# The last output tile of a TensorE-bound kernel: two equal column pieces, or a wide and a narrow one with its copy on VectorE

## The chip, the cores and the metric

The kernel runs on one core of one Trainium2 chip. The metric is the time of one execution on the device, in microseconds (us); lower is better. Each kernel is executed several times, and kernels of one set run on the same chip in turn with the kernel before.

The *execution time* is what is compared. The *span* is the stretch from the first to the last of the program's own instructions in the profile. The profile prints the span to 0.1 us; where two or three decimals are given below, they come from the trace behind it. "Outside the span" below is the execution time of the profiled execution minus the span of that same execution.

## The reference

Normalised linear attention over 8 batches of 576 tokens, 8 heads of 64, and then two matrix products with an ELU between them (4608 tokens, 512 to 2048 to 512):

```python
kv  = einsum('bhsd,bhse->bhde', k, v)
out = einsum('bhsd,bhde->bhse', q, kv)
rms = sqrt(mean(out * out, axis=-1, keepdims=True) + 1e-06)
x   = (out / rms * g_norm)            # then (b, h, s, d) -> (b*s, h*d)
h   = x @ w_in                        # 4608 x 2048
g   = where(h > 0, h, exp(min(h, 0)) - 1)
y   = g @ w_out                       # 4608 x 512
```

## The kernel before

The tokens are worked off in nine groups of 512; in each, TensorE makes `h` (lines with `h_ps`), ScalarE and VectorE make the ELU, and TensorE makes the output (`o_ps`). The change touches only the end: the output of the last group. Its four tiles of 128 tokens x 512 columns need 16 accumulating matmuls each. The last tile is already cut into two column pieces of 256, so that the copy and the store of the first piece overlap the matmuls of the second:

```python
    rows = out.rearrange("(i l s) f -> l s i f", l=2, s=S)
    pieces = [(j, slice(0, DM)) for j in range(J - 1)]
    pieces += [(J - 1, slice(0, DM // 2)), (J - 1, slice(DM // 2, DM))]
    for j, cols in pieces:
        n = cols.stop - cols.start
        ps = ps_m2.tile([P, DM], FP32, name="o_ps", tag="mm2")[:, 0:n]
        for f in range(FC):                       # FC = 16
            nc.tensor.matmul(ps, lhsT=gT[B][:, f, j * P : j * P + P],
                             rhs=w_out_sb[:, f, cols], start=(f == 0), stop=(f == FC - 1))
        sb = outp.tile([P, DM], FP32, name="o_last", tag="o_last", bufs=5)[:, 0:n]
        nc.scalar.copy(sb, ps)
        for l, eng in enumerate((nc.sync, nc.scalar)):
            eng.dma_start(out=rows[l, G:S, j, cols], in_=sb[l * 64 : l * 64 + 64, :])
```

Two small VectorE instructions of the start play a part later:

```python
    one = const.tile([1, 1], FP32, name="one")
    nc.vector.memset(one, 1.0)
    # ... read by one small matmul near 8 us
```

Of the kernel before, what the change touches and what calls it, by code (L numbers as in the profile page):

```python
# [8 lines left out]
FP32 = mybir.dt.float32  # L9
# [7 lines left out]
def kernel(  # L17
# [13 lines left out]
    nc = tc.nc  # L31
    P = 128

    B, H, S, D = q.shape
    DM = H * D
    DF = moe_w_in.shape[1]
    NPAIR = H // 2
    J = 4
# [13 lines left out]
    outp = ctx.enter_context(tc.tile_pool(name="outp", bufs=3))  # L52
# [452 lines left out]
    for s in range(2):  # L505
# [7 lines left out]
        out=g_row,  # L513
        in_=bass.AP(tensor=g_norm.tensor, offset=g_norm.offset, ap=[[1, 1], [0, 2], [1, 64]]),
# [160 lines left out]
    for l in range(2):  # L675
        ls = slice(l * 64, l * 64 + 64)
        nc.gpsimd.tensor_copy(
            out=bd_kv[ls, 0].rearrange("p (s u) e -> p u s e", s=2)[:, :, :, ls], in_=kv0[ls]
# [117 lines left out]
            ahead["qd"]()  # L796
    rows = out.rearrange("(i l s) f -> l s i f", l=2, s=S)
    pieces = [(j, slice(0, DM)) for j in range(J - 1)]
    pieces += [(J - 1, slice(0, DM // 2)), (J - 1, slice(DM // 2, DM))]
    for j, cols in pieces:  # L800
        n = cols.stop - cols.start
        ps = ps_m2.tile([P, DM], FP32, name="o_ps", tag="mm2")[:, 0:n]
        for f in range(FC):
            nc.tensor.matmul(  # L804
                ps,
                lhsT=gT[B][:, f, j * P : j * P + P],
                rhs=w_out_sb[:, f, cols],
                start=(f == 0),
                stop=(f == FC - 1),
            )  # L810
        sb = outp.tile([P, DM], FP32, name="o_last", tag="o_last", bufs=5)[:, 0:n]
        nc.scalar.copy(sb, ps)
        for l, eng in enumerate((nc.sync, nc.scalar)):
            eng.dma_start(out=rows[l, G:S, j, cols], in_=sb[l * 64 : l * 64 + 64, :])

# [29 lines left out]
```

## Time and profile before

| what | value | view |
|---|---|---|
| execution time | 287.24 us, median of 3 (287.07 to 287.27) | times |
| TensorE busy | 98% of the span | busy table |
| last matmul ends (modelled) | 283.62 us | trace |
| last copy, ScalarE, 256 columns | 283.66 us, 0.372 us | timeline, groups |
| last two stores issued | 284.06 us | timeline |
| both landed | 286.27 us | trace |
| end of the span | 287.24 us | trace |

So 3.62 us lie between the end of the last matmul and the end of the span. They are called the *tail* here.

These are lines of the page of the kernel before: span, TensorE's busy time, the granted TensorE clock in 40 slices (tenths of full speed), and the chain that ended last, by engine.

```profile
span 287.2 us, 4859 instructions
...
PE 280.8 (98%) x2001; PEld 134.8 (47%) x2001; DVE 168.8 (59%) x220; ACT 144.1 (50%) x205; POOL 53.5 (19%) x94
...
PEclk9689999999999999999999999999999999999999
...
PE 97%; ACT 1%; DVE 0%; issue 0%
```

TensorE is the bound. Note the 6 and the 8 at the start of the clock row: in this one execution the granted clock was 0.50 from about 9.8 to 16.7 us (0.68 and 0.84 as means of those two slices). That execution took 289.14 us, not 287.24, so its early part is not typical; its tail is.

The end of the timeline of the kernel before; the columns are start in us, duration in us, engine, line, operation, operands, and in brackets the idle time before it and what ended that.

```profile
start us, us, engine line op out<-in xcount [idle before <-releaser]
...
281.91 0.37 ACT L812 COPY o_last<-o_ps 128x256 f32<-128x256 f32 x1 [1.16 <-PE o_ps L804]
282.31 0.50 ACTq L814 DMA_DIRECT2D out_dram<-o_last  x1
283.66 0.37 ACT L812 COPY o_last<-o_ps 128x256 f32<-128x256 f32 x1 [1.38 <-PE o_ps L804]
284.06 0.50 ACTq L814 DMA_DIRECT2D out_dram<-o_last  x1
```

The two copies start 1.75 us apart, which is 16 matmuls of 109 ns. ScalarE waits for TensorE before each.

From the groups of instructions of the kernel before (busy us, mean ns of one, idle before): what copies of other sizes take.

```profile
L812 ACT COPY o_last<-o_ps 128x512 f32<-128x512 f32 x3 | 1.8, 586 | 8.2 <-PE o_ps L804 8.2
...
L812 ACT COPY o_last<-o_ps 128x256 f32<-128x256 f32 x2 | 0.7, 372 | 2.5 <-PE o_ps L804 2.5
L579 DVE COPY r<-bank 128x512 f32<-128x512 f32 x1 | 0.7, 692 | 0.8 <-PE bank L567 0.8
...
L608 DVE COPY g_col<-bank 128x1 f32<-128x1 f32 x1 | 0.2, 157 | 0.3 <-PE bank L601 0.3
```

And the stores of the last tiles among its DMA issues (size, median us from issue to landing):

```profile
out_dram<-o_last SPq DMA_DIRECT2D x3, 128.0 KB, 2.4
out_dram<-o_last ACTq DMA_DIRECT2D x3, 128.0 KB, 2.7
...
out_dram<-o_last SPq DMA_DIRECT2D x2, 64.0 KB, 1.9
out_dram<-o_last ACTq DMA_DIRECT2D x2, 64.0 KB, 2.2
```

Halving the bytes of a store took only 0.5 us off 2.4 to 2.7. Most of it did not change with the size.

### The profile page before, as it was taken

How to read it: one execution, taken by the hardware profiler on the slowest of the kernel's cores; microseconds unless marked ns; L12 is line 12 of the kernel's file. 1: busy time of each engine (PE TensorE's matmuls, PEld its weight loads, DVE VectorE, ACT ScalarE, POOL GpSimd, SP SyncE). 2: the span in 40 equal slices, each digit the busy share in tenths (PEclk: the TensorE clock that was granted, in tenths of full speed). 3: DMA queues.
4: the chain of work that ended last, by engine and by line, in shares of the span. 5: the costliest groups of instructions: out<-in, count | busy, mean ns of one | idle time of the engine just before them, and what ended most of it. 6: DMA issues, size and time to landing. Idle time of an engine off the chain costs nothing.

```text
span 287.2 us, 4859 instructions
## 1 busy us (share of the span) xinstructions
PE 280.8 (98%) x2001; PEld 134.8 (47%) x2001; DVE 168.8 (59%) x220; ACT 144.1 (50%) x205; POOL 53.5 (19%) x94
## 2 busy tenths in 40 slices
PE   7999999999999999999999999999999999999994
PEld 3444445444554454445444544454444444444444
DVE  5348752589368657755775477538764776444400
ACT  3569744685496455445543554345534553333311
POOL 7726302431421151005200520012000000000000
PEclk9689999999999999999999999999999999999999
DMA  7999999795896599258925892544251213010122
GB/s 197 204 206 203 207 204 156 222 195 116 136 176 76 147 130 219 39 146 108 219 59 147 100 232 50 147 91 137 47 139 36 85 29 109 0 75 0 73 73 73
DMA packets 55961, 35.96 MB, mean 125 GB/s; under 512 B 32772, under 2 KB 53508, under 8 KB 55940
## 3 DMA queue, kind: packets, MB, share of 16 engines
q0 software_dynamic: 20192, 17.30, 38.9%
q1 hardware_dynamic: 35348, 17.83, 24.6%
q10 hardware_dynamic: 400, 0.52, 0.5%
q8 instruction: 15, 0.25, 0.3%
q14 instruction: 6, 0.05, 0.0%
HBM read 36.70 MB, written 9.44 MB: 161 GB/s over the span
## 4 chain that ended last, share of the span: by engine, by line
PE 97%; ACT 1%; DVE 0%; issue 0%
PE h_ps L399 42%; PE o_ps L446 39%; PE o_ps L804 5%; PE bank L527 3%; PE at L208 2%; PE at L177 2%; PE kv_ps L177 1%; PE at L659 1%; PE h_ps L659 1%; PE bank L567 1%; PE bank L196 1%; PE at L306 0%; PE bank L583 0%; PE at L217 0%; PE at L188 0%; PE se_ps L208 0%
## 5 line engine op out<-in xcount | busy, mean ns | idle before, releaser
L399 PE MATMUL h_ps<-xT,w_in_sb 128*128 128x512 bf16 x560 | 130.9, 379 | 0.0
L446 PE MATMUL o_ps<-w_out_sb,gT 128*128 128x512 bf16 x512 | 120.5, 379 | 0.0
L411 ACT ACTIVATE elu_e<-h_ps 128x1024 bf16<-128x1024 f32 (+1 forms) x75 | 73.0, 982 | 81.8 <-PE h_ps L399 80.1
L399 PEld LDWEIGHTS <-w_in_sb 128*128 128x128 bf16 x560 | 53.6, 98 | 62.0 <-issue 0.2
L430 DVE TENSOR_TENSOR gT<-elu_e,h_ps 128x1024 bf16<-128x1024 bf16 (+1 forms) x66 | 76.3, 1157 | 6.9
L446 PEld LDWEIGHTS <-gT 128*128 128x128 bf16 x512 | 49.8, 98 | 59.0
L422 DVE TENSOR_SCALAR elu_e<-elu_e 128x1024 bf16<-128x1024 bf16 (+1 forms) x76 | 32.7, 430 | 70.7 <-ACT elu_e L411 70.5
L459 ACT COPY o_sb<-o_ps 128x512 f32<-128x512 f32 x32 | 18.6, 587 | 16.4 <-PE o_ps L446 16.4
L232 DVE TENSOR_REDUCE ss<-sq 128x16 f32<-128x1024 bf16 x16 | 19.3, 1218 | 8.7 <-ACT sq L227 8.7
L227 ACT ACTIVATE sq<-at 128x1024 bf16<-128x1024 f32 x14 | 14.3, 1024 | 12.4 <-PE at L208 9.9
L151 POOL COPY q_bf<-q_pk 128x512 bf16<-128x512 bf16 x24 | 14.5, 632 | 28.7 <-DMA q_pk<-in_q_dram 28.7
L242 DVE TENSOR_TENSOR xs<-at,ss 128x1024 bf16<-128x1024 f32 x14 | 17.1, 1218 | 1.2 <-ACT ss L239 1.2
L804 PE MATMUL o_ps<-w_out_sb,gT 128*128 128x512 bf16 (+1 forms) x80 | 14.1, 337 | 0.0
L125 POOL COPY gate<-qT 1x1 bf16<-1x1 bf16 x6 | 1.1, 184 | 63.2 <-DMA qT<-q_bf 63.2
L104 POOL DMA_DIRECT2D q_pk<-in_q_dram x14 | 10.7, 772 | 2.9 <-issue 1.9
L804 PEld LDWEIGHTS <-gT 128*128 128x128 bf16 x80 | 7.8, 98 | 6.4 <-DVE gT L430 0.4
L527 PE MATMUL bank<-zeros 128*128 128x512 bf16 x19 | 8.5, 587 | 1.2 <-DVE zeros L502 1.2
L118 POOL DMA_DIRECT2D k_pk<-in_k_dram x12 | 8.4, 700 | 5.8 <-DMA w_in_sb<-in_moe_w_in_dram 2.9
L417 ACT ACTIVATE elu_h<-h_ps 128x1024 bf16<-128x1024 f32 x9 | 9.2, 1019 | 0.0
L177 PEld LDWEIGHTS <-k_pk 64*64 64x64 bf16 x576 | 7.0, 110 | 4.2 <-issue 4.0
L208 PEld LDWEIGHTS <-qT 128*128 128x128 bf16 x112 | 7.3, 98 | 3.5 <-issue 0.5
L118 POOL DMA_DIRECT2D v_pk<-in_v_dram x12 | 8.4, 698 | 2.3 <-DMA w_in_sb<-in_moe_w_in_dram 1.8
(71 smaller groups left out, 116.4 us busy)
## 6 DMA issues: line engine op xcount, KB each, us to landing
out_dram<-o_sb SPq DMA_DIRECT2D x16, 512.0 KB, 3.0
q_pk<-in_q_dram POOLq DMA_DIRECT2D x14, 256.0 KB, 5.2
k_pk<-in_k_dram POOLq DMA_DIRECT2D x6, 576.0 KB, 8.2
v_pk<-in_v_dram POOLq DMA_DIRECT2D x6, 576.0 KB, 10.5
w_in_sb<-in_moe_w_in_dram POOLq DMA_DIRECT2D x4, 512.0 KB, 11.1
w_out_sb<-in_moe_w_out_dram POOLq DMA_DIRECT2D x4, 512.0 KB, 14.7
st_q<-in_q_dram SPq DMA_DIRECT2D x2, 512.0 KB, 4.7
st_q<-in_q_dram SPq DMA_DIRECT2D x16, 64.0 KB, 2.5
```

The source lines that it names most:

```text
L118: nc.gpsimd.dma_start(out=raw[name, b].rearrange("p h j d -> p h (j d)")[:, hs], in_=in_[:, hs])
L177: nc.tensor.matmul(kv_ps[l * 64 : l * 64 + 64, s, u * 64 : u * 64 + 64], lhsT=bf["k", T][rows, j, 2 * u + l, :], rhs=bf["v", T][rows, j, 2 ...
L232: nc.vector.reduce_sum(out=ss, in_=sq.rearrange("p c (h e) -> p (c h) e", h=H), axis=AX.X)
L242: nc.vector.tensor_tensor(out=xs.rearrange("p c (h e) -> p (c h) e", h=H), in0=se_ps.rearrange("p c (h e) -> p (c h) e", h=H), in1=ss.to_b ...
L399: nc.tensor.matmul(h_ps[a][:, cs], lhsT=w_in_sb[:, c, f * P : f * P + P], rhs=x(c, cs), start=(c == 0), stop=(c == KC - 1),)
L411: nc.scalar.activation(e[:, lo:hi, :], ps, AF.Exp)
L422: nc.vector.tensor_scalar(out=e[:, lo:hi, :], in0=e[:, lo:hi, :], scalar1=1.0, scalar2=1.0, op0=ALU.min, op1=ALU.subtract,)
L430: nc.vector.tensor_tensor(out=gT[T][:, 2 * i + lo : 2 * i + hi, :], in0=e[:, lo:hi, :], in1=h, op=ALU.add if relu else ALU.max,)
L446: nc.tensor.matmul(o_ps[T, j], lhsT=gT[T][:, f, j * P : j * P + P], rhs=w_out_sb[:, f, :], start=(f == 0), stop=(f == FC - 1),)
L459: nc.scalar.copy(o_sb[T][:, j % 2, :], o_ps.pop((T, j)))
L527: nc.tensor.matmul(ps, lhsT=zeros[:, 0:P], rhs=zeros, start=True, stop=True)
L804: nc.tensor.matmul(ps, lhsT=gT[B][:, f, j * P : j * P + P], rhs=w_out_sb[:, f, cols], start=(f == 0), stop=(f == FC - 1),)
```

## The change

The intent is a shorter tail: a narrower last piece needs a shorter copy and a smaller last store. VectorE makes the last copy, because ScalarE would still be busy with the copy and the DMA issue of the wide piece.

```diff
-    pieces += [(J - 1, slice(0, DM // 2)), (J - 1, slice(DM // 2, DM))]
+    pieces += [(J - 1, slice(lo, hi)) for lo, hi in ((0, 384), (384, 512))]
 ...
-        sb = outp.tile([P, DM], FP32, name="o_last", tag="o_last", bufs=5)[:, 0:n]
-        nc.scalar.copy(sb, ps)
+        sb = outp.tile([P, DM], FP32, name="o_last", tag="o_last", bufs=6)[:, 0:n]
+        if cols.stop == DM and n < DM:
+            nc.vector.tensor_copy(out=sb, in_=ps)
+        else:
+            nc.scalar.copy(sb, ps)
```

## The prediction

> **What bounds the kernel now.** TensorE. The busy table has PE at 280.8 of 287.2 us (98%), and the chain of waits is 97% PE. Only the tail after the last matmul is not PE. In the timeline the last tile's two 256-column pieces end 1.745 us apart (ScalarE copies at 281.91 and 283.66), 109 ns per matmul. After the last matmul: copy 0.372 us from 283.66, two DMA issues at 284.06 (SP and ACT queues), landing near 286.27 (1.9 to 2.2 us after issue, DMA table), then about 0.97 us of closing semaphores to 287.24. Of these 3.6 us only the copy and the data part of the DMA can shrink.
>
> **What the change removes, adds, moves.**
> 1. PE: 32 matmuls stay 32. A 128-wide one takes 56 ns elsewhere (the chain: eight in 0.45 us), so weight loads keep up. [...]this trace agrees at 512 (1.73 us / 8 = 216 ns), 256 (109) and 128 (56), so 384 should be 162.5. Estimate: 16 x (162.5 + 56) = 3.50 us against 3.49. Neutral; last matmul still ends at about 283.63.
> 2. Last copy: 128 columns instead of 256, on VectorE. Two VectorE copies from PSUM in this trace: 512 f32 columns 692 ns, 1 column 157 ns; so about 290 ns for 128 (a 128-column cast takes 288). Against 372: saves 0.08 us. On ScalarE the 128 columns would take about 265 ns (586 for 512, 372 for 256), but ScalarE would be busy: the 384 copy (about 0.48 us) plus its DMA issue (0.50) reach past the 0.90 us of the last piece by about 0.15 us. VectorE, idle since 272.6 us, avoids that. The engine choice only protects the gain.
> 3. Last DMA: half the bytes, 512-byte rows. Data of a 512-wide piece moved in about 1.14 us, of a 256-wide in about 0.73 (the trace's packets); so about 0.55 for 128: up to 0.18 us less. But the 384 piece, issued near 283.32, moves from about 284.4 to 285.4, and the last piece, issued near 283.98, starts moving near 285.1: they overlap by about 0.3 us on the same DMA engines, which may eat most of that. Net 0 to 0.15 us.
> 4. A sixth output buffer; nothing else moves in the instruction order.
>
> **On the critical path:** 0.08 us of copy and about 0.06 us of DMA. Sum about -0.14 us, 0.05% of the run, less than the spread of three runs (0.20 us).
>
> **Predicted time:** 287.10 us; 8 in 10 between 286.85 and 287.35. Faster by over 2%: 0.005; within 2%: 0.99; slower by over 2%: 0.005.
>
> **What would show each step right:** PE busy and the start of the last copy unchanged within 0.03 us (1); a VectorE copy of 280 to 300 ns as last link of the chain, with its DMA issues at about 283.98, no wait on a busy queue (2); landing of the last pieces at 286.05 to 286.25, with packets of the 384 piece still moving when the last ones begin (3).
>
> **What would make it wrong:** weight loads not keeping up through sixteen 128-wide matmuls (each 10 ns over 56 costs 0.16 us); the 384 piece's data holding up the last one by over 0.3 us, which turns the gain into a small loss; run-to-run drift larger than the effect.

The 162.5 ns for 384 columns stays as an estimate: it lies midway between the 109 ns at 256 columns and the 216 ns at 512 in the profile before.

## The result

| | before | changed |
|---|---|---|
| execution time, median of 6 | 287.24 us (287.07 to 287.38) | 287.38 us (287.21 to 287.46) |
| ratio changed / before, 95% interval | | 1.0005 (0.9992 to 1.0018) |

A ratio here and below is the mean time of one kernel's fast runs over that of the other's of the same rounds, so not quite the ratio of the medians. The result is not the gain of 0.14 us that was predicted, and it lies 0.03 us above the predicted range.

The page of the changed kernel, the same rows:

```profile
span 285.4 us, 4859 instructions
...
PE 277.7 (97%) x2001; PEld 133.2 (47%) x2001; DVE 168.4 (59%) x221; ACT 143.7 (50%) x204; POOL 53.3 (19%) x94
...
PEclk9999999999999999999999999999999999999999
...
PE 88%; DMA 10%; issue 0%; ACT 0%; DVE 0%; POOLq 0%
```

The span is 1.8 us shorter, but that must not be credited to the change: this profile caught full clock all through, the other did not. With full clock the chain starts with the loading of the weights ("DMA 10%") instead of TensorE work. That is a property of the execution. The kernel before, profiled again later (run before_again below), had full clock too, and its page shows the shorter span and the same chain:

```profile
span 285.5 us, 4859 instructions
...
PE 88%; DMA 10%; issue 0%; ACT 0%; POOLq 0%
```

The end of the timeline of the changed kernel:

```profile
start us, us, engine line op out<-in xcount [idle before <-releaser]
...
281.09 0.48 ACT L815 COPY o_last<-o_ps 128x384 f32<-128x384 f32 x1 [2.01 <-PE o_ps L804]
281.60 1.39 ACTq L817 DMA_DIRECT2D out_dram<-o_last  x2
281.98 0.29 DVE L813 COPY o_last<-o_ps 128x128 f32<-128x128 f32 x1 [11.10 <-PE o_ps L804]
```

Its stores of the last tile, to set beside those of before:

```profile
out_dram<-o_last SPq DMA_DIRECT2D x1, 96.0 KB
out_dram<-o_last ACTq DMA_DIRECT2D x1, 96.0 KB, 2.4
out_dram<-o_last SPq DMA_DIRECT2D x1, 32.0 KB, 2.0
out_dram<-o_last ACTq DMA_DIRECT2D x1, 32.0 KB, 2.1
```

The steps of the tail came out close to the prediction, except for one DMA issue (below). The last tile takes TensorE 3.657 us against 3.656 (matmuls of 384 columns start 162.5 ns apart, those of 128 columns 56 ns). The VectorE copy takes 292 ns. From the issue on the ACT queue to the moment when SyncE sees both stores landed, 2.154 us pass against 2.212. The tail is 3.474 us against 3.620. So 0.15 us were gained where they were sought, and the execution is still not shorter. Something else must cost about as much or more.

The exception is the last DMA issue on the ACT queue. The timeline above merges it with the issue before it; alone it is

```profile
282.31 0.68 ACTq L817 DMA_DIRECT2D out_dram<-o_last  x1
```

It took 0.68 us, against 0.50 in the kernel before. The prediction had "no wait on a busy queue" here. What that costs shows in split_act below.

A first pointer was in the runs themselves. The six executions of the changed kernel took 1.99 to 2.06 us longer than their spans (spans known to 0.1 us), where the one profiled execution of the kernel before took 1.90 us longer.

### The profile page after: what moved, and what is told of

Same layout as the page of the kernel before. It is cut to its first block, busy times and chain, and to the rows that moved or that the text cites. A ratio compares the mean times of both kernels' runs of the same rounds, so it can differ in the third digit from the quotient of the medians.

```text
span 285.4 us, 4859 instructions
## 1 busy us (share of the span) xinstructions
PE 277.7 (97%) x2001; PEld 133.2 (47%) x2001; DVE 168.4 (59%) x221; ACT 143.7 (50%) x204; POOL 53.3 (19%) x94
## 4 chain that ended last, share of the span: by engine, by line
PE 88%; DMA 10%; issue 0%; ACT 0%; DVE 0%; POOLq 0%
PE h_ps L399 39%; PE o_ps L446 39%; DMA w_out_sb<-in_moe_w_out_dram 6%; PE o_ps L804 5%; DMA w_in_sb<-in_moe_w_in_dram 3%; PE at L208 2%; DMA k_pk<-in_k_dram 2%; PE at L177 2%; PE at L306 0%; PE at L217 0%; PE se_ps L208 0%; ACT bd_kv L356 0%; PE xt_ps L306 0%; DVE o_last L813 0%; POOLq L832 0%
## 5 line engine op out<-in xcount | busy, mean ns | idle before, releaser
L422 DVE TENSOR_SCALAR elu_e<-elu_e 128x1024 bf16<-128x1024 bf16 (+1 forms) x76 | 31.8, 419 | 71.6 <-ACT elu_e L411 71.6
L804 PE MATMUL o_ps<-w_out_sb,gT 128*128 128x512 bf16 (+2 forms) x80 | 14.1, 337 | 0.0
L430 DVE TENSOR_TENSOR gT<-elu_e,elu_h 128x1024 bf16<-128x1024 bf16 x9 | 6.6, 735 | 2.9 <-ACT elu_h L417 2.4
```

Of the source, the lines that this page charges most:

```text
L422: nc.vector.tensor_scalar(out=e[:, lo:hi, :], in0=e[:, lo:hi, :], scalar1=1.0, scalar2=1.0, op0=ALU.min, op1=ALU.subtract,)
L430: nc.vector.tensor_tensor(out=gT[T][:, 2 * i + lo : 2 * i + hi, :], in0=e[:, lo:hi, :], in1=h, op=ALU.add if relu else ALU.max,)
L804: nc.tensor.matmul(ps, lhsT=gT[B][:, f, j * P : j * P + P], rhs=w_out_sb[:, f, cols], start=(f == 0), stop=(f == FC - 1),)
```

## The experiments

The theories as they stood, in order:

- A: the total is only scatter of the part before the tail; with more runs the 0.14 us gain would show.
- B: something before the tail became slower, for example by moved addresses of the larger pool.
- C: the time outside the span became longer. Within it, C1: it depends on how many instructions VectorE has; C2: it depends on VectorE working late.

dve_plus9, dve_plus2, dve_plus5, dve_plus129, dve_plus128 and act_extra were single looks, whose state is unknown; only their tail and their time outside the span are used, not their totals. "Tail" is from the modelled end of the last matmul to the end of the span. Medians are of the same set; "before" in each set is that set's own runs of the kernel before, on the same chip. The five sets ran on chips 15, 8, 11, 14 and 15.

### First set: is it scatter, is it the pool, does the tail count at all?

**before_again**: no edit.

> The kernel before, unchanged, against itself. It measures how far two sets of runs of one kernel lie apart. Theory A (the change shortens the tail by 0.14 us, and the +0.14 us of the first timing is scatter of the part before the tail): medians of the two sets may differ by up to 0.15 us, single runs spread over 0.2 to 0.4 us. Theory B (the changed kernel really is about 0.14 us slower): the two sets agree within 0.05 us. In the profile, both theories: from the start of the last copy to the end 3.58 us, as in the first profile.

Measured: 287.40 us median of 6 against 287.35 of 11 runs of the same kernel; ratio 1.0012 (0.9966 to 1.0058). Tail 3.595 us. Outside the span 1.797 us. Single runs spread from 287.04 to 291.19 us. The medians of one kernel agree within 0.05 us here, but single runs go astray far more. Theory B falls here in its general form, as far as one profile of each kernel can tell: with full clock the last matmul ended at 281.95 us in this run and at 281.95 us in the first profile of the changed kernel.

**after_again**: the changed kernel, no edit.

> The changed kernel, unchanged, timed with more rounds. Theory A: 0.0 to 0.3 us below the kernel before (-0.14 expected), with the scatter of single runs larger than that. Theory B (something outside the tail costs about 0.28 us and outweighs the tail): +0.14 us again, interval clear of zero. Profile, both: VectorE copy 290 ns, from the start of the last copy to the end 3.44 us.

Measured: 287.60 us of 6 against 287.35; ratio 1.0010 (0.9971 to 1.0048). Tail 3.467 us, again 0.14 us shorter. Outside the span 1.992 us, 0.20 more than in the run of the kernel before beside it. The second set of timings has the changed kernel above the kernel before too, though no interval excludes equality.

**six_buffers**

```diff
-        sb = outp.tile([P, DM], FP32, name="o_last", tag="o_last", bufs=5)[:, 0:n]
+        sb = outp.tile([P, DM], FP32, name="o_last", tag="o_last", bufs=6)[:, 0:n]
```

> The kernel before with six output buffers in place of five, nothing else; the sixth is never used. Theory A: within 0.1 us of the kernel before. Theory B, in the form that the larger pool or its moved addresses cost the time: +0.14 to +0.28 us. Tail from the last copy's start to the end unchanged at 3.58 us.

Measured: 287.40 us against 287.35; ratio 0.9999 (0.9967 to 1.0032). Tail 3.601 us, outside the span 1.768 us. The buffer is not the cause; theory B falls in that form too.

**one_piece**

```diff
-    pieces += [(J - 1, slice(0, DM // 2)), (J - 1, slice(DM // 2, DM))]
+    pieces += [(J - 1, slice(0, DM))]
```

> The last tile in one piece of 512 columns, copied by ScalarE: the same term of the sum made larger the other way, as a check that a longer tail reaches the total one for one. Copy 0.586 us in place of 0.372 (+0.21), the data of the last DMA 1.14 us in place of 0.73 (up to +0.4): tail 4.1 to 4.2 us from the start of the last copy, total +0.5 to +0.65 us. Both theories expect this; if the total moved by less than +0.3 us, the tail would not be on the critical path as assumed.

Measured: 287.97 us against 287.35 (+0.62); ratio 1.0025 (0.9988 to 1.0061), so the total alone is not clear of noise. The tail is 4.374 us, 0.77 more than the 3.61 us of before. Outside the span 1.772 us. By the medians a longer tail reaches most of the total, so a shorter one should as well.

### Second set: what lies outside the span

**split_act**: the last copy of the changed kernel back on ScalarE.

```diff
-        if cols.stop == DM and n < DM:
-            nc.vector.tensor_copy(out=sb, in_=ps)
-        else:
-            nc.scalar.copy(sb, ps)
+        nc.scalar.copy(sb, ps)
```

> The changed kernel with its last copy on ScalarE instead of VectorE. So far the profile shows the tail 0.14 us shorter with the change, while the total is not shorter; what the total has beyond the profiled span was 2.0 us in all runs of the changed kernel, and 1.77 to 1.90 us in the four kernels without the VectorE copy. Theory C: that part outside the span belongs to the VectorE copy and hides the gain. It expects here 1.77 to 1.90 us outside the span. Theory A (scatter only) expects no pattern. Tail, both: the last copy can't start before ScalarE has issued the 384 piece's DMA, so it starts about 0.15 us after its last matmul and takes 265 ns; tail counted from the last matmul about 0.1 us longer than with VectorE, about as before.

Measured: 287.09 us of 5 against 287.26 of 11; ratio 0.9988 (0.9966 to 1.0010). Outside the span 1.768 us. Tail 3.499 us, better than expected. The end of its timeline:

```profile
280.97 0.48 ACT L812 COPY o_last<-o_ps 128x384 f32<-128x384 f32 x1 [2.01 <-PE o_ps L804]
281.48 0.50 ACTq L814 DMA_DIRECT2D out_dram<-o_last  x1
282.02 0.27 ACT L812 COPY o_last<-o_ps 128x128 f32<-128x128 f32 x1 [0.57 <-PE o_ps L804]
282.31 0.55 ACTq L814 DMA_DIRECT2D out_dram<-o_last  x1
```

The last matmul ended at 281.82 us and the copy began at 282.02, once the DMA issue was off ScalarE's queue (281.48 + 0.50). So ScalarE really is late, by 0.16 us (the usual gap is 0.04). But its copy is 26 ns shorter, and the tail is still 0.11 us shorter than before. VectorE's part in the change is worth only about 0.03 us of tail. The record shows why it is so little. In the changed kernel the last issue on the ACT queue starts 0.13 us earlier after the last matmul (0.36 us against 0.49), but it takes 0.68 us instead of 0.55, so both end 1.04 us after the last matmul. In these traces this issue took 0.67 to 0.68 us when it started 0.71 us after the issue before it (five runs), 0.55 us at 0.84 us and 0.50 us at 0.95 us or more. The reason isn't shown.

**halves_dve**

```diff
 (from the changed kernel)
-    pieces += [(J - 1, slice(lo, hi)) for lo, hi in ((0, 384), (384, 512))]
+    pieces += [(J - 1, slice(lo, hi)) for lo, hi in ((0, 256), (256, 512))]
```

> Two pieces of 256 as in the kernel before, the last copied by VectorE (and six buffers). VectorE copy 256 columns about 425 ns (157 + 256 x 1.045), against 372 on ScalarE: tail +0.05 us, 3.61 to 3.64 us from the copy's start. Theory C: 2.0 us outside the span, total +0.25 us. Theory A: no pattern, total +0.05 us.

Measured: 287.59 us of 6 against 287.26; ratio 1.0015 (0.9990 to 1.0041). Copy 425 ns, tail 3.663 us, outside the span 2.008 us. The cost outside came with VectorE's copy, not with the sizes of the pieces.

**dve_extra**: one more VectorE instruction that has nothing to do with the tail.

```diff
 (from the kernel before, ahead of "rows = ...")
+    nc.vector.memset(const.tile([P, 1], FP32, name="unused"), 0.0)
```

> The kernel before with one more VectorE instruction, a memset of one unused column that nobody waits for, placed after VectorE's last real work; tail 3.56 to 3.58 us as before. Theory C1 (VectorE's instruction count is what costs outside the span): 2.0 us outside, total +0.2 us. Theory C2 (that VectorE is still at work when the kernel ends): 1.77 to 1.90 us outside, total unchanged. Theory A: unchanged.

Measured: outside the span 2.013 us. VectorE's last lines in its timeline:

```profile
269.97 1.22 DVE L430 TENSOR_TENSOR gT<-elu_e,h_ps 128x1024 bf16<-128x1024 bf16 x1
271.14 0.06 DVE L797 MEMSET unused<- 128x1 f32 x1
```

VectorE is done at 271.2 us of a span of 285.9, and nobody waits for the memset. Yet the time outside the span grew just as it does with the VectorE copy. C2 falls: late work is not the cause. The total was 287.74 us of 5 against 287.26, more than expected; in the profiled execution 0.3 us of it is a later last matmul (282.25 us, against 281.95 in before_again). That is taken here for scatter of the part before the tail. It isn't shown: four of the five spans were 285.7 us or more, against a median of 285.5 for the kernel before in this set.

**dve_even**: the changed kernel with one VectorE memset moved away. This one went wrong.

```diff
 (from the changed kernel)
-    nc.vector.memset(one, 1.0)
+    nc.gpsimd.memset(one, 1.0)
```

> The changed kernel with one early VectorE memset of one element moved to GpSimd, so that VectorE has as many instructions as in the kernel before. Tail 3.43 to 3.44 us as in the changed kernel. Theory C1: 1.77 to 1.90 us outside the span, total -0.14 us against before. Theory C2: 2.0 us outside, total +0.05 us. Theory A: -0.14 us give or take 0.15.

Measured: 301.61 us, 14 us slower. The memset had to queue behind the DMA issues of GpSimd: in the profile it ran at 20.30 us, right after a DMA issue of 0.71 us that began at 19.59. A small matmul reads it, at 8.4 us in the kernel before and at 20.4 us here. The lines of that matmul's view: what its engine sat idle for, and who waited for it.

```profile
its engine sat idle before it (us, times) until:
  POOL one L508: 24.3, 2
who waited for it (us, times):
  DVE g_col L608: 12.7, 1
```

The 24.3 us are 12.2 us of the weight load and 12.1 us of the matmul, at the same time. The total is useless, an error of the experiment. Its tail (3.455 us) and the time outside the span (1.767 us) can still be read, and they favour C1. The edit was repeated in a clean form.

### Third set: the count, and better versions

**dve_const**

```diff
 (from the changed kernel)
-    one = const.tile([1, 1], FP32, name="one")
-    nc.vector.memset(one, 1.0)
+    one = nc.const_aps.tensor(1.0, (1, 1), FP32)
```

> The changed kernel with the one-element VectorE memset of 1.0 left out; its reader takes the 1.0 that the framework has already put in memory at the start. VectorE then has 309 instructions in the trace as in the kernel before, and still makes the last copy. (The attempt before, with that memset moved to GpSimd, stalled TensorE for 12 us at the start and its total says nothing; its tail was 3.42 us and the part outside the span 1.77 us.) Theory C1: 1.77 us outside the span, tail 3.43 us, total 0.10 to 0.20 us below the kernel before. Theory C2 (late VectorE work costs): 2.0 us outside, total +0.05 us.

Measured: 287.14 us of 5 against 287.29 of 9; ratio 0.9988 (0.9967 to 1.0009). Tail 3.469 us, outside the span 1.782 us. With one VectorE instruction fewer at the very start of the program, the changed kernel shows its gain in the medians.

**dve_plus9**: nine unused memsets in the place of the one of dve_extra.

```diff
 (from the kernel before; n = 9, and below n = 2, 5, 128, 129)
+    unused = const.tile([P, n], FP32, name="unused")
+    for c in range(n):
+        nc.vector.memset(unused[:, c : c + 1], 0.0)
```

> The kernel before with nine more VectorE memsets that nobody waits for, in the place of the one of the earlier experiment (318 VectorE instructions). If each instruction costs outside the span: 1.77 + 9 x 0.24 = 3.9 us. If it is a step at one more instruction than before (309 to 310): 2.0 us, as with one more.

Measured: outside the span 1.796 us. Neither of the two forms expected: nine more instructions cost nothing outside the span, though one more costs 0.24 us. So it is neither a price for each instruction nor a step that stays.

**act_extra**

```diff
 (from the kernel before)
+    nc.scalar.copy(const.tile([P, 1], FP32, name="unused"), eps_col)
```

> The kernel before with one more ScalarE instruction (a copy of one column that nobody waits for), VectorE at 309. If the cost outside the span comes with VectorE's own count: 1.77 us. If it comes with the program's total count or with any engine: 2.0 us.

Measured: outside the span 1.810 us. One more instruction in total, or one more on ScalarE at this place, does not bring the cost; with dve_extra beside it, the effect belongs to VectorE's count.

**act_352**: an attempt to beat both kernels without VectorE.

```diff
 (from split_act)
-    pieces += [(J - 1, slice(lo, hi)) for lo, hi in ((0, 384), (384, 512))]
+    pieces += [(J - 1, slice(lo, hi)) for lo, hi in ((0, 352), (352, 512))]
```

> A version meant to beat both: pieces of 352 and 160 columns, all copied by ScalarE. The last piece's matmuls take [...]1.11 us, longer than ScalarE needs for the copy of 352 (0.45 us) and the DMA issue (0.50) with their gaps, so the last copy (292 ns) starts as soon as its matmuls end, 0.04 us after. Theory C1: 1.77 us outside the span, tail from the last matmul about 3.44 us against 3.60 before and 3.50 with 384 and 128 on ScalarE; total 0.15 to 0.2 us below the kernel before.

The 1.11 us stands as an estimate from the 56 ns at 128 columns and the 109 ns at 256 of the profile before: about 69 ns at 160, times 16. In the run the two last copies start 1.11 us apart.

Measured: 287.08 us of 5 against 287.29 of 9; ratio 0.9984 (0.9960 to 1.0008). Outside the span 1.776 us, tail 3.414 us.

```profile
280.82 0.45 ACT L812 COPY o_last<-o_ps 128x352 f32<-128x352 f32 x1 [1.80 <-PE o_ps L804]
281.30 0.50 ACTq L814 DMA_DIRECT2D out_dram<-o_last  x1
281.93 0.29 ACT L812 COPY o_last<-o_ps 128x160 f32<-128x160 f32 x1 [0.66 <-PE o_ps L804]
282.25 0.50 ACTq L814 DMA_DIRECT2D out_dram<-o_last  x1
```

The last matmul ended at 281.89 us, and the copy started 0.04 us later: the last piece is just wide enough for ScalarE to have its DMA issue behind it, and the last issue takes 0.50 us again. In the tail it gives the whole gain of the change, with no VectorE at all.

### Fourth and fifth set: one unlucky count, or a step that recurs?

**dve_plus2**: n = 2.

> The kernel before with two unused VectorE memsets (311 VectorE instructions). Outside the span so far: 309 gives 1.77 to 1.80 us (one first look 1.90), 310 gives 1.99 to 2.01 in four kernels, 318 gives 1.80. If only a single count is hit: 1.77 us. If a stretch of counts from 310 up to somewhere under 318 is hit, with the cost fading as the count grows: 1.9 to 2.0 us.

Measured: outside the span 2.100 us.

**dve_plus5**: n = 5.

> The same with five unused memsets (314 VectorE instructions). Single count: 1.77 us. Fading stretch: 1.8 to 1.95 us.

Measured: outside the span 1.865 us. With 2.10 at two and 1.80 at nine, it is a stretch of counts over which the cost fades.

**dve_plus129**: n = 129, which is 128 more than dve_extra.

> The same with 129 unused memsets (438 = 310 + 128 VectorE instructions[...]). If the cost comes[...]: 2.0 us again. If not[...]: 1.77 to 1.80 us. The memsets take about 9 us of VectorE time and end before the last matmul, so the tail stays at 3.56 to 3.60 us.

To test: 2.0 us if the step recurs after 128 instructions, 1.77 to 1.80 us if it does not.

Measured: outside the span 1.994 us, as with one more. The 129 memsets took 3.03 us in its timeline, not about 9.

**dve_plus128**: n = 128.

> The kernel before with 128 unused VectorE memsets (437 = 309 + 128), one fewer than the run that gave 1.99 us outside the span. If the step recurs each 128 instructions, it lies between 437 and 438 as between 309 and 310: 1.77 to 1.80 us. If many instructions cost something of themselves: 1.95 to 2.0 us, as with 129.

Measured: outside the span 1.776 us. The step lies between 437 and 438 as it lies between 309 and 310, and it is not the number of instructions as such that costs.

**after_plus8**: the changed kernel, with eight unused VectorE memsets more.

> The changed kernel with eight unused VectorE memsets more (318 VectorE instructions): adding work to take the cost away. The theory[...]: 1.78 to 1.82 us outside the span, tail 3.43 to 3.44 us, total 0.08 to 0.2 us below the kernel before, although it executes more. If the theory is wrong and the late VectorE copy itself costs: 2.0 us outside, total at or above the kernel before.

"The theory" is C1, that the number of VectorE's instructions sets the cost, with the counts measured so far.

Measured: 287.10 us of 5 (286.95 to 287.33) against 287.26 of 9 (287.15 to 287.55); ratio 0.9996 (0.9982 to 1.0010). Outside the span 1.777 us, tail 3.413 us. VectorE in its timeline:

```profile
270.65 0.17 DVE L799 MEMSET unused<- 128x1 f32 x8
281.80 0.29 DVE L816 COPY o_last<-o_ps 128x128 f32<-128x128 f32 x1 [10.98 <-PE o_ps L807]
```

The page of this profiled execution, which took 286.95 us, begins:

```profile
span 285.2 us, 4867 instructions
```

The late copy on VectorE is still there, and the cost outside the span is gone, because eight idle instructions were added. This is the sharpest test of C1 and it passes. (Its tail is 0.05 to 0.06 us shorter than in the other profiles of the changed kernel; why isn't shown.)

### The count and the time outside the span

"Count" is the number of VectorE's records in the trace, those of its sequencer (semaphores and closing instructions) included; the x220 and x221 of the pages leave these out. Each value is of the one profiled execution.

| VectorE count | kernels | outside the span, us |
|---|---|---|
| 309 | before_again, six_buffers, one_piece, split_act, dve_even, dve_const, act_extra, act_352 | 1.80, 1.77, 1.77, 1.77, 1.77, 1.78, 1.81, 1.78 |
| 309 | before, first profile (289.14 us) | 1.90 |
| 310 | changed, after_again, halves_dve, dve_extra | 2.01, 1.99, 2.01, 2.01 |
| 311 | dve_plus2 | 2.10 |
| 314 | dve_plus5 | 1.87 |
| 318 | dve_plus9, after_plus8 | 1.80, 1.78 |
| 437 | dve_plus128 | 1.78 |
| 438 | dve_plus129 | 1.99 |

The step does not rest on these single profiles. Every execution from the second timing on, and the six of the changed kernel in the first timing, has its span to 0.1 us. The 23 executions at count 310 (four builds) lie between 1.97 and 2.07 us outside the span, mean 2.02. The 75 at count 309 without dve_even (the kernel before and six edits) lie between 1.73 and 1.85 us, mean 1.78; the five of dve_even between 1.72 and 1.94. The five of after_plus8, at 318, lie between 1.75 and 1.83.

The runs show: the time outside the span jumps by about 0.2 us when VectorE's stream grows from 309 to 310 instructions, is largest at 311, has faded at 318, and jumps again 128 instructions later. Of the two instructions tried, it doesn't matter which one is added: the tail copy, or an idle memset ahead of it.

What the runs do not show is the mechanism, since these 0.2 us lie outside the span. The page has DMA queues of the kind "instruction"; for the kernel before and for the changed kernel it counts the same packets on them in the span (queue, packets, MB, share of the DMA engines' time):

```profile
q8 instruction: 15, 0.25, 0.3%
q14 instruction: 6, 0.05, 0.0%
```
```profile
q8 instruction: 15, 0.25, 0.3%
q14 instruction: 6, 0.05, 0.1%
```

In these two traces each of the 6 packets of queue 14 is of 8192 bytes, each of the 15 of queue 8 of 16384, and none comes after the end of the span. At count 318 one was seen there:

```profile
q14 instruction: 1, 0.01, 0.8%
```

(dve_plus9, DMA from 286 us on; the span ends at 285.7.) Yet dve_plus9 has only 1.80 us outside the span, and the changed kernel, without such a packet, has 2.01. So these packets do not explain the cost, and its cause is not shown. A period of the cost shorter than 128 that divides it, such as 16, 32 or 64, was not excluded either. One profile at count 309 (the first, with the disturbed clock) read 1.90 us and stays unexplained; the clock alone is not it, as four other executions of the kernel before with a mean clock of 0.98 to 0.99 read 1.74 to 1.79 us.

## Why the prediction was right or wrong

**What bounds the kernel, and the tail's place on the critical path: right.** TensorE is 97 to 98% busy, and a tail made 0.77 us longer (one_piece) made the median of the total 0.62 us longer.

**Matmuls neutral: right.** 3.657 us for the last tile against 3.656. For 384 columns 162.5 ns was estimated, midway between the measured 109 and 216; the trace shows 162.5.

**Copy 290 ns, 0.08 us saved: right.** 292 ns against 372.

**Last store, about 0.06 us saved: right.** 2.154 us against 2.212 from issue to seen landed. In the trace the 384 piece's packets were still moving when the last ones began, for 0.12 us instead of the 0.3 foreseen. The check "no wait on a busy queue" failed, by an issue of 0.68 us in place of 0.50.

**"The engine choice only protects the gain": wrong in size, and in what it left out.** ScalarE was late by 0.16 us, where 0.15 was foreseen, but its copy is shorter, VectorE's earlier start is lost again in the longer DMA issue, and so the tail is only about 0.03 us longer than with VectorE (3.499 against 3.467 to 3.474). And the engine choice adds one instruction to VectorE's stream.

**The step that failed: "Sum about -0.14 us", with "nothing else moves in the instruction order" behind it.** The sum took the change of the tail for the change of the execution time. The order in the program was read correctly; that the *number* of VectorE's instructions matters outside the profiled span was not thought of. The missing term measures +0.22 us (2.00 us in two profiles of the changed kernel, less 1.78 in before_again and six_buffers), or +0.24 by the means of all executions at 310 and 309. With the tail's -0.13 (3.470 less 3.605, means of the changed kernel's two and of before, before_again and six_buffers) the sum is +0.09 to +0.11 us. The medians show +0.14 and +0.25 us, which agrees as far as scatter allows. Take the term away, by one VectorE instruction fewer (dve_const) or eight more (after_plus8), and the medians are 0.15 and 0.16 us below the kernel before, as the tail alone would have it.

**The range was too narrow.** The prediction set its width of 0.5 us beside three runs that agreed within 0.20 us. Later runs of the kernel before spread from 286.95 to 291.19 us.

None of the timings alone decides a difference of 0.15 us: every interval above contains 1, except for one that tells only of dve_even's mistake. What decides is that the tail repeats within some hundredths of a microsecond from profile to profile, and that the times outside the span of the 23 executions at count 310 and of the 80 at 309 in these sets do not overlap, while the part before the tail wanders by several tenths or more.

## What to carry to other kernels

At the end of a TensorE-bound kernel, make the last piece as narrow as the engine that copies it allows. Here that was 160 columns on ScalarE (3.41 us of tail against 3.61): its matmuls last 1.11 us, the copy and the DMA issue of the piece before 0.45 and 0.50. With 128 columns they last 0.90 us (16 of 56 ns), the copy and the issue before 0.48 and 0.50, and ScalarE was 0.16 us late. This was tried with three cuts only (256 and 256, 384 and 128, 352 and 160). The f32 copies of these tails out of `o_ps` took 266 ns at 128 columns, 372 at 256, 479 at 384 and 586 at 512 on ScalarE, and 292 at 128 and 425 at 256 on VectorE. When a change gains in the profile and not in the execution time, subtract the span from the execution time of the same run before looking for a cause inside the profile. For effects of 0.1%, add or remove a few idle instructions on the engine whose count changed, as a control, before crediting or blaming the change itself.
